# Adding the lower parts of float64 weights by accumulating transfers instead of identity products

## The chip, the cores and the metric

The kernel runs on one core of a Trainium2 chip. A core has a matrix engine (TensorE, PE in the profile), a vector engine (VectorE, DVE), a scalar engine (ScalarE, ACT), a general engine (GpSimd, POOL) and a queue engine that issues transfers (SyncE, SP); 16 DMA engines move the data between DRAM and the on-chip memory SBUF. Each engine takes its instructions in the order of the program and waits on semaphores for the others. PE writes into the accumulators (PSUM); ACT and DVE read them out. The metric is device microseconds (us) of one launch, lower is better.

## The reference

Two attentions in a row, then a gated layer. `q`, `k`, `v` are float32 `[8, 8, 576, 64]` (batch, head, sequence, width), `p` holds 32 packed queries for each head.

```python
p_packed = sm_attn(p, k, v)
out = sm_attn(q, p_packed, p_packed)          # scale 1/8, softmax, 576 x 32 scores for each head
x = out.transpose(0, 2, 1, 3).reshape(8, 576, 512)
h = relu(x @ w_in)                            # w_in  [512, 1024], float64
conv = sum_k conv_w[k] * shift(h, k - 1)      # conv_w [3, 1024], float64, along the sequence
return ((h * sigmoid(conv)) @ w_out).astype(float32)   # w_out [1024, 512], float64
```

The three weights come as float64, since a float32 array was multiplied by a float64 scalar. [...]

## The kernel before, in words

**Tiling.** There are 16 groups `g` of four heads (two to a batch). `attention(g)` runs the first attention on the 32 packed queries of four heads, and the second one with its results. `packed_weight(b, hf)` multiplies the packed results of batch `b` into half `hf` of `w_in`, so that `ffn1(b, j)`, j = 0 to 7, makes 128 of the 1024 channels of `h` straight from the second attention's weights, applies the convolution and the gate, and leaves the result in `hgt`. `ffn2(m)`, m = 0 to 35, multiplies 128 rows of it with `w_out`: 24 products of 512 columns, three for each of 8 chunks.

**Split precision.** The large products run on float32r, a rounded form of float32. Their operands are split into a high part (rounded) and a low part (what the rounding left), and three products high·high, high·low, low·high are added. So `ffn2` needs `wo_hi` and `wo_lo`, and a tile `xhi` and `xlo` of its input; `ffn1` needs `ghi`, `glo` and `a2hi`, `a2lo`.

**The weights.** `w_in` and `w_out` are cut into four tiles each, `weight(0)` to `weight(3)` and `weight(4)` to `weight(7)`, of 128 x 1024 numbers (1 MB as float64). Below, W0 to W7 are these tiles. `load_weight(i)` brings one into a staging area (a part of `hgt[1]`, or `stage`). `f64_parts` then takes the upper words on ACT (line 267), shifts and masks them on DVE (lines 269 and 271) into the main part `t` and the factor `e`, and multiplies the lower words by `e` on DVE (line 273) into `lo`, a part of `wo_lo`. The number is t + lo. Before the change, `lo` has the sign turned, and PE makes the sum: the identity times `t` plus the negative identity times `lo`, and for W4 to W7 also minus `hi`, the rounded copy of `t` that ACT has made on line 318 (line 325, two halves of 512 columns). ACT copies the result out of the accumulators on line 329: to `w_in_sb` for W0 to W3, to `wo_lo` for W4 to W7. Events name the stages: ("wd", i) loaded, ("wp", i) staging free, ("ws", i) scratch in `wo_lo` free, ("w", i) tile ready. `packed_weight(b, 0)` needs W0 and W1, `packed_weight(b, 1)` W2 and W3, and `ffn2(0)` W4 to W7.

**The order.** Each of these functions is a stream of steps; a step is the work of one engine. `ORDER` is a table written out in the source: pairs of base-36 digits, each the number of the stream whose next step is issued. What each engine does, and in what order, is fixed by it. `Flow` walks through the table, with a model of the times of its own, for one purpose alone: where it expects PE to stand idle, it puts idle products of the identity (`warm`, line 243), as long as the first `ffn2` has not been issued. Tokens (`gw`, `x`, `big` and others) stand for buffers and must be free before a step that takes them.

**What the steps before `ffn2(0)` are.** On DVE the table of before has 106 steps ahead of line 679 of `ffn2(0)`: the three steps on lines 269, 271 and 273 for each of W0 to W7, the softmax steps of groups 0 to 3 and the first of group 4, two transposes on line 417, lines 650, 654 and 660 for the eight `ffn1(0, j)`, and line 650 of `ffn1(1, 0)`. On PE they are 76 steps ahead of `ffn2(0)`, the eight of line 325 among them.

Of the kernel before, what the change touches and what calls it, by code (L numbers as in the profile page):

```python
# [18 lines left out]


ORDER = (
    "003k3m04020303040304080b0b04050b0j053k3l06060c0c0j0c0506013q0g06050j0c0e063r0o3u0k0k0r3k3k070e3k0e073k3r3r060906"
    "0k0k0e0f0f3r06060e0m0m3k3k0a06063v3v0r0r3s060s0s3v0e3n0s0m0d3w0i060q3v0e0e0m0s0d0d0e060606060n0h40060d3r3t3t3t0z"
    "0z0m3r0u0u0u0z3x0e3t0n3v3v170e06063t3t0l0l3x0e0m0m3x3y0e0e3x0e0v0e060e0e46460u0u0l0m4641410e410v413x0l0m0p46170m"
    "0m3x3z3z0m170t3z47410w0m0u0e0e423z10471f0t0u0m0m41410t0t470u0u0u0u3z47480m0u0m120u434848121249490u490m144843480u"
    "49434a4a123z4849484a4a490u494a0u444b12453z43454a4a0m4b150x4c4c1f1f4g4c4c124d4b4b43434g4g4c0u4b4d4c4c4d4d4b4b0m0m"
    "4d434g4e4e4d0u0u454d4f4f0u454h4h4h4f4f4e4e454h4f4f4i4i4e4e45184i1a4f4e1c4i1313456e6e4j4j124j0y1a4k4k4k4i4j4k1212"
    "164i4i6e6e4k6f1a6e6e6e6e6e4k6e1n1g1a1a114l6e4l4l6f4j121i4k1i1b1b1a124j4j4l1212191i4m4m1a4m1j4m4m6f4n1a4n3o1l1a6g"
    "6f6f1n6f6f1a4q4n1n124m4l4l6g1a4m4l4n1j121a1d1s1k6f6f6f1v6f6f4o4o1o4n4p4o4o4o124p4p4q204p4p6h4q6h4o6g1i1i6g1v6g6g"
    "1v1a6g6g6g6g4n236g6g12124p4n121q1i1i4r4p1q4o23231a1q1w126i1a1a6i1a121a1a6h6h6h6h6h6h1q1q6h6h4r6h1t1e6h6e1y1y6j1a"  # L30
    "1a1r1r1q1q1y246i6i6i6i6i1h4r4s4s4s4s4t4t2b1m1y6i4t1z4s2b2b291z4t4t6i1y1i1i284s4t2626261y1i1i4u4u6i6i6i4s6j4t4v1y"
    "4v4u4v1p1i1i4v1u3p212j4u4u2c4w2g6k6k1q6j6j6j266j6j6j6j6j4w1q1i4w4w1i1i4u6j262e274u2e4w4w501q1q4v1i4w4v2j2j6k2o6k"
    "6k6k6k2e6l4v2k1q1q6l1y6k4x4x501y6k6k6k6k4y2a271i1i4y4y1x4y4y4z4z1q1q226l6l1y1y262r4z6m6m264x4x4x6l2e2e2r6l6l6l1i"
    "1i1q1q4z4z4x4x1q6l6l512m2r6l4y4z4z4y1q1q6n51501q6m6m6m6l6j6m6m6m6m6m6m6m2h2f26526n6n1y2m2f516n6o52521y2m1y535354"
    "5426546n256n6n6n6o5252521y5454541y52262e2w6n6n5326546p6n555555262d261y26531y5a536o2m566o6o6o26556p55262z2e2e5353"
    "36561y5a556o556o565626566o6o6o5a2e6o6q56566q265757576p1y6p2z6p5758582s582p596p1y59596p6p6p6p572m2657266p2z585858"
    "572n5959595b2e2u2u582m592e262n6q2i6q6q6q6q2u6q2u6q6q6p2x6r6r2e2m375b6q6q2e2e5c5b2l305c5c5c6r375d2e6s5d5d5e6r5e5c"
    "2q2v5d5d375c5e5c5e5d2u5d6r6r6r5e5e2e5e3f6r6r6r2m2m5f5f5f5g5g6s5h2v2m2u325f2e5f2e5g5g2m345g6t6r6r5h6t5f5f6s6s5g5h"
    "6s2u2m5h5h2e6s6s6s6s5g6s6s6s5i5i6t6t5h2e5i2m385i6t6t2m6u6t6t2u2u6t6t322m2m2m2t6u5i5j2m326t5j3f5k5k5j6n6t2e5h5l5l"
    "6v5i2m2m6v335k326u6u6u2m6u6u6u6u6u6u5i5j5j5m5m5j5l5m3f5j326v6v5n5n5n5m3c5m5m5n5n5o5o2y6v5m332u32325o5n3a3a3g3a6v"  # L40
    "5p5p6v6v6v326v5n5o5o6w6w316v5o5q5q3a2u5o3b6w6w6v6u356w6w5r5q3a5p5q32325p5p2u2u3b5q5r6x5r5r5p5p3i5u5q5u3a326w6w6w"
    "6w6w6w6x5r5q395s5s3i325r2u2u2u6y2u6y6x6x6x6x6x6x6x5s6x3i3a3j3j6x6z5t5t5t5s2u5r5s32322u32326y6y6y6y3i6y6y6y6z6y5s"
    "2u3i6y323e3a3a5v3d5v2u5s5t5t5t5u3i3a6z5t6x7032323270326z6z6z6z6z6z6z6z3i5v5w5w5w6z5w5w5x5x5x5x5x5y5y705y3a5y3i3i"
    "705w5x5x71703h5y5w3a717070707070705z6y70605y5z5z5y5z726060713i3i5z5z6064643i3i3a5z7261617171717171613a3a3i717171"
    "717362623a3a3a6160603a613i3i3a723a6072737272727272727263626363636161643i7474633i73737373737373737373653i3i746262"
    "74636274747474637474743i6275666674726667676775686666666667677575756975756565687668687575756867676868766975756969"
    "6a6a6a6b7676696a6a6b6969766a6b6b6b6b6a76767676766c77776c76766d78786c6d6d7777777777777777776b6d6d6d6c6c6c6c6d7779"
    "797878787878787878787979797a7a79797979797a79797b7b7a7a7a787a7a7a7a7a7a7b7b7b7c7c7b7b7b7b7b7b7b7c7c7c7c7c7d7d7c7c"
    "7c7c7c7d7d7d7d7d7d7d7d7d7d"
)  # L50


# [133 lines left out]
def tile_packed_attention_conv_gate(  # L186
# [71 lines left out]
    def f64_parts(tiles, raw, m, after=(), take=(), sets=None):

        pair = raw.rearrange("r (c t) -> r c t", t=2)  # L260
        up = pair[:, :, 1].bitcast(I32)
        low = pair[:, :, 0].bitcast(U32)
# [4 lines left out]
        nc.scalar.activation(out=e, in_=up.bitcast(F32), func=AF.Prelu, scale=F64_REBIAS, alpha=-(2.0**32))  # L267
# [1 line left out]
        nc.vector.tensor_scalar(out=ti, in0=ei, scalar1=3, scalar2=None, op0=ALU.logical_shift_left)
# [28 lines left out]
    def weight(i):  # L298

        c, cols, src, st = weight_tile(i)  # L300
        hi, lo = (w[:, 2 * (i % 4) : 2 * (i % 4) + 2, :].rearrange("r c f -> r (c f)") for w in (wo_hi, wo_lo))
# [8 lines left out]
        after = [("wd", i), "minus"] + ([("ws", i - 4)] if i >= 4 else [])  # L310
        if src.dtype != F32:
            yield from f64_parts(tiles, st, DFF, after, [token], [("wp", i)])
        else:
            yield Step("DVE", 0, after=after, take=[token])
            parts.append((ident, st))
        if i >= 4:
            yield Step("ACT", 905)
            nc.scalar.copy(out=hi, in_=parts[0][1])
# [4 lines left out]
        for hf in range(2):
            for k, (w, x) in enumerate(parts):
                nc.tensor.matmul(  # L325
                    out=s[:, hf, :], lhsT=w, rhs=x[:, 512 * hf : 512 * hf + 512], start=k == 0, stop=k == len(parts) - 1
                )
# [1 line left out]
        nc.scalar.copy(out=w_in_sb[:, c : c + 2, cols] if i < 4 else lo.rearrange("r (c f) -> r c f", c=2), in_=s)  # L329
# [151 lines left out]
    def attention(g):  # L481
        G = grp[g]
        yield Step("PE", 556, after=[("pT", g), ("kT", g)] + [("s1", g - 1)] * (g > 0), take=["big", "a1"], give=["kT", "pT"], sets=[("s1", g)], cols=1152, tiled=True)
        t = score(G["pT"], G["kT"], g)
# [2 lines left out]
        nc.vector.tensor_reduce(out=nm, in_=t[:, :, :SH], axis=AX.XY, op=ALU.max, negate=True)  # L487
# [3 lines left out]
        nc.scalar.activation(
# [70 lines left out]
        G["a2"] = (hi, lo)  # L562

    def sums(g):
        yield Step("DVE", 69, after=[("sm", g)])
# [1 line left out]
        nc.vector.tensor_scalar(out=rs, in0=grp[g]["sm"], scalar1=EPS, scalar2=None, op0=ALU.add)
# [1 line left out]
        nc.vector.reciprocal(out=rs, in_=rs)
# [188 lines left out]
```

## Time and profile before

| | |
|---|---|
| time, median of 2 runs | 421.76 us (421.48 to 422.05) |
| the profiled execution's own time | 422.01 us |
| its span, first to last instruction | 420.2 us |
| PE busy / DVE / ACT / POOL | 410.4 / 343.6 / 316.3 / 1.6 us |
| mean granted clock of PE | 0.994 |
| transfers | 47.21 MB; on the GpSimd queue 0.02 MB |

The span is cut into 40 slices on the profile's page: PE is busy at 90% or more in all but the first and the last, DVE in the third to the 25th at 80% or more and falling behind them, ACT at 90% from about 40 us to 80 us. Matmuls are pipelined and their ends are modelled, so consecutive starts tell more about PE than durations: line 695 has rows of about 400 ns that start 233 ns apart. A row of DVE overlaps the one behind it by about 70 ns in the same way.

### The profile page before, as it was taken

How to read it: one execution, taken by the hardware profiler on the slowest of the kernel's cores; microseconds unless marked ns; L12 is line 12 of the kernel's file. 1: busy time of each engine (PE TensorE's matmuls, PEld its weight loads, DVE VectorE, ACT ScalarE, POOL GpSimd, SP SyncE). 2: the span in 40 equal slices, each digit the busy share in tenths (PEclk: the TensorE clock that was granted, in tenths of full speed). 3: DMA queues.
4: the chain of work that ended last, by engine and by line, in shares of the span. 5: the costliest groups of instructions: out<-in, count | busy, mean ns of one | idle time of the engine just before them, and what ended most of it. 6: DMA issues, size and time to landing. Idle time of an engine off the chain costs nothing.

```text
span 420.2 us, 8196 instructions
## 1 busy us (share of the span) xinstructions
PE 410.4 (98%) x3347; PEld 324.4 (77%) x3347; DVE 343.6 (82%) x488; ACT 316.3 (75%) x505; POOL 1.6 (0%) x13
## 2 busy tenths in 40 slices
...
GB/s 254 381 383 309 181 256 82 43 85 153 100 168 180 112 165 137 81 111 58 129 103 127 27 79 111 2 108 111 56 50 27 25 2 75 27 25 25 51 50 51
DMA packets 135621, 47.21 MB, mean 112 GB/s; under 512 B 119700, under 2 KB 127892, under 8 KB 135584
## 3 DMA queue, kind: packets, MB, share of 16 engines
...
q0 software_dynamic: 32, 0.02, 0.1%
...
## 4 chain that ended last, share of the span: by engine, by line
PE 85%; ACT 4%; DVE 1%; issue 0%; ACTq 0%
PE fo L695 45%; PE big L633 23%; PE sm L695 4%; PE big L444 4%; PE big L581 3%; PE sm L507 2%; PE big L498 2%; PE big L325 1%; ACT hgt L658 0%; ACT wo_lo L329 0%; ACT hbuf L644 0%; PE sm L523 0%; PE idle L243 0%; PE sm L471 0%; ACT L658 0%
## 5 line engine op out<-in xcount | busy, mean ns | idle before, releaser
L695 PE MATMUL fo<-wo_hi,xhi 128*128 128x512 f32 x264 | 107.6, 408 | 0.7 <-ACT o L700 0.7
L695 PE MATMUL fo<-wo_hi,xlo 128*128 128x512 f32 x264 | 104.3, 395 | 0.0
L695 PE MATMUL fo<-wo_lo,xhi 128*128 128x512 f32 x264 | 104.3, 395 | 0.0
L679 DVE TENSOR_TENSOR xlo<-hgt,xhi 128x1024 fp32r<-128x1024 f32 (+1 forms) x40 | 44.0, 1105 | 23.6 <-ACT xhi L676 23.4
L695 PEld LDWEIGHTS fo<-wo_hi,xhi 128*128 128x128 f32 x264 | 49.7, 188 | 15.8 <-ACT o L700 1.9
L650 DVE SCALAR_TENSOR_TENSOR hgt<-hbuf,cw,hgt 128x576 f32<-128x576 f32 x64 | 51.5, 808 | 10.9 <-ACT hgt L648 10.5
L695 PEld LDWEIGHTS fo<-wo_hi,xlo 128*128 128x128 f32 x264 | 49.6, 188 | 11.9
L695 PEld LDWEIGHTS fo<-wo_lo,xhi 128*128 128x128 f32 x264 | 49.7, 188 | 9.1
L633 PE MATMUL big<-a2hi,ghi 128*128 128x288 f32 x256 | 55.8, 299 | 0.0
L633 PE MATMUL big<-a2lo,ghi 128*128 128x288 f32 x256 | 54.8, 295 | 0.0
L633 PE MATMUL big<-a2hi,glo 128*128 128x288 f32 x256 | 54.5, 294 | 0.0
L644 ACT ACTIVATE hbuf<-big 128x576 f32<-128x576 f32 x64 | 41.8, 655 | 14.5 <-PE big L633 13.1
L654 DVE SCALAR_TENSOR_TENSOR hgt<-hbuf,cw,hgt 128x576 f32<-128x576 f32 x64 | 51.7, 810 | 1.1
L658 ACT ACTIVATE hgt<-hgt 128x576 f32<-128x576 f32 x64 | 43.2, 684 | 10.6 <-DVE hgt L654 10.5
L660 DVE TENSOR_TENSOR hgt<-hgt,hbuf 128x576 f32<-128x576 f32 x64 | 47.4, 748 | 4.6 <-ACT hgt L658 4.4
L648 ACT ACTIVATE hgt<-hbuf,cw 128x576 f32<-128x576 f32 x64 | 49.5, 778 | 1.0
L700 ACT COPY o<-fo 128x512 f32<-128x512 f32 x33 | 19.4, 587 | 36.9 <-PE fo L695 31.0
L633 PEld LDWEIGHTS big<-a2hi,ghi 128*128 128x128 f32 x256 | 42.2, 188 | 6.1 <-issue 0.9
L633 PEld LDWEIGHTS big<-a2hi,glo 128*128 128x128 f32 x256 | 41.0, 188 | 0.0
L633 PEld LDWEIGHTS big<-a2lo,ghi 128*128 128x128 f32 x256 | 40.9, 188 | 0.0
L676 ACT CAST xhi<-hgt 128x1024 fp32r<-128x1024 f32 (+1 forms) x40 | 38.2, 961 | 2.5 <-DVE hgt L660 1.6
L487 DVE TENSOR_REDUCE nm<-big 128x1 f32<-128x576 f32 x16 | 12.0, 749 | 14.9 <-PE big L444 14.8
...
## 6 DMA issues: line engine op xcount, KB each, us to landing
out_dram<-o SPq DMA_DIRECT2D x36, 256.0 KB, 2.2
...
hgt<-in_moe_w_in_dram SPq DMA_DIRECT2D x3, 1024.0 KB, 11.3
hgt<-in_moe_w_out_dram SPq DMA_DIRECT2D x3, 1024.0 KB, 7.5
...
```

The costliest lines, as they stand in the source:

```text
L444: nc.tensor.matmul(out=o.rearrange("c (j r) -> c j r", r=NR) if by_block(g) else o, lhsT=lhs[r, 32 * i : 32 * i + 32], rhs=rhs[r, :, h, :] ...
L633: nc.tensor.matmul(out=t[:, hf, :SH], lhsT=w[:, gg, js], rhs=x[:, hf * SH : (hf + 1) * SH], start=n == 0, stop=n == 3 * NG - 1,)
L644: nc.scalar.activation(out=h[:, 1 : S + 1].rearrange("c (f s) -> c f s", f=2), in_=t[:, :, :SH], func=AF.Relu)
L648: nc.scalar.activation(out=d, in_=h[:, 1 : S + 1], func=AF.Copy, scale=cw[:, NJ + j : NJ + j + 1])
L650: nc.vector.scalar_tensor_tensor(out=d, in0=h[:, 0:S], scalar=cw[:, j : j + 1], in1=d, op0=ALU.mult, op1=ALU.add)
L654: nc.vector.scalar_tensor_tensor(out=d, in0=h[:, 2 : S + 2], scalar=cw[:, 2 * NJ + j : 2 * NJ + j + 1], in1=d, op0=ALU.mult, op1=ALU.add)
L658: nc.scalar.activation(out=d, in_=d, func=AF.Sigmoid)
L660: nc.vector.tensor_tensor(out=d, in0=d, in1=h[:, 1 : S + 1], op=ALU.mult)
L676: nc.scalar.copy(out=hi[:, :, o], in_=src)
L679: nc.vector.tensor_tensor(out=lo[:, :, o], in0=src, in1=hi[:, :, o].bitcast(F32), op=ALU.subtract)
L695: nc.tensor.matmul(out=t, lhsT=x[:, c, :], rhs=w[:, c, :], start=c + i == 0, stop=c == NJ - 1 and i == 2)
L700: nc.scalar.copy(out=o, in_=t)
```

## The change

The sum t + lo is made by a transfer that the GpSimd queue issues, from SBUF to SBUF, which adds `lo` to what lies at its destination (512 KB of it for each tile). `lo` keeps its sign. For W0 to W3, `t` is written straight into `w_in_sb`, the transfer adds `lo` to it there, and nothing else is to be done. For W4 to W7, `t` lies in the `xhi` buffer; behind the transfer ACT makes `hi` from it, and a new step on DVE makes `lo = t - hi`. The PE steps of line 325 and the ACT copies of line 329 go. The order table is a new one (1521 steps where there were 1525), with two added rules on who must be issued before whom in `attention` and `sums`. `w_in` tiles W1 and W0 are now loaded in the order W1, W0, ahead of the first `v`.

```diff
 ORDER = (
...
+    ACCUMULATE = 3000
...
-        nc.vector.scalar_tensor_tensor(... scalar=2.0**-52 if rest.dtype == F32 else -(2.0**-52), ...)
+        nc.vector.scalar_tensor_tensor(... scalar=2.0**-52, ...)
...
         def tiles():
-            t, e = (wk.tile([128, DFF], F32, name="tmp", tag=tag) for tag in tags)
-            parts.extend([(ident, t), (minus, lo)])
-            return t, e, lo
+            t, e = (wk.tile([128, DFF], F32, name="tmp", tag=tag) if i >= 4 or tag == tags[1] else None for tag in tags)
+            whole.append(pair(t) if i >= 4 else w_in_sb[:, c : c + 2, cols])
+            return whole[0], pair(e), pair(lo)
+
         if src.dtype != F32:
-            yield from f64_parts(tiles, st, DFF, after, [token], [("wp", i)])
+            yield from f64_parts(tiles, st, DFF, after, [token], [("wp", i)], pair)
+            yield Step("POOL", ACCUMULATE, give=[token] * (i < 4), sets=[("ws", i)] + [("w", i)] * (i < 4))
+            nc.gpsimd.dma_start(out=whole[0], in_=pair(lo), accum_op=ALU.add)
...
         if i >= 4:
-            yield Step("ACT", 905)
-            nc.scalar.copy(out=hi, in_=parts[0][1])
-            parts.append((minus, hi))
-        ns = 2 * (864 + 234 * (len(parts) - 1))
-        yield Step("PE", ns, take=["big"], give=[token], sets=[("ws", i)], cols=2 * (1536 + 512 * len(parts)))
-        s = big()
-        for hf in range(2):
-            for k, (w, x) in enumerate(parts):
-                nc.tensor.matmul(
-                    out=s[:, hf, :], lhsT=w, rhs=x[:, 512 * hf : 512 * hf + 512], start=k == 0, stop=k == len(parts) - 1
-                )
-        yield Step("ACT", 905, give=["big"], sets=[("w", i)])
-        nc.scalar.copy(out=w_in_sb[:, c : c + 2, cols] if i < 4 else lo.rearrange("r (c f) -> r c f", c=2), in_=s)
+            yield Step("ACT", 905, after=after)
+            nc.scalar.copy(out=pair(hi), in_=whole[0])
+            yield Step("DVE", 1135, give=[token], sets=[("w", i)] + [("wp", i)] * (src.dtype == F32))
+            nc.vector.tensor_tensor(out=pair(lo), in0=whole[0], in1=pair(hi).bitcast(F32), op=ALU.subtract)
```

Read as steps, the new table does this. On PE the same 68 other steps stand ahead of `ffn2(0)`, and one more, the transpose of line 471 for group 7. On DVE 109 steps stand ahead of line 679 of `ffn2(0)`: those of before without line 650 of `ffn1(1, 0)`, and the four new subtractions. On ACT the eight copies of line 329 and line 601 of `packed_weight(1, 1)` are gone from ahead of line 676 of `ffn2(0)`, and three short steps have come there (lines 468, 518 and 526). The GpSimd queue gets eight transfers, in the order W0, W1, W2, W3, W5, W4, W6, W7. The loads on SP begin with k0, p0, p1, k1, q0, W1, W0, v0, where they began with k0, p0, q0, k1, v0, W0 (the letter is the array, the number the group or tile).

More of the change, by code (lines that the diff above doesn't have):

```diff
@@ L27 @@
[L27 to L46, printed above, removed]
@@ L47 @@
-    "6a6a6a6b7676696a6a6b6969766a6b6b6b6b6a76767676766c77776c76766d78786c6d6d7777777777777777776b6d6d6d6c6c6c6c6d7779"
-    "797878787878787878787979797a7a79797979797a79797b7b7a7a7a787a7a7a7a7a7a7b7b7b7c7c7b7b7b7b7b7b7b7c7c7c7c7c7d7d7c7c"
-    "7c7c7c7d7d7d7d7d7d7d7d7d7d"
+    "003m3k3n08030403030b040404023s3q0105063k3k3k06063u3k3k0c060c0b0g0b0c3r063k0c3k0e0e090j0j3t0a0o050i050e0j3r3r073t"
+    "073r3v3v060606050e0k3w0h0e06060k0f0k0f3v3v0k0d0d3r0m0606063t0m3t3t3v0d0d0e3l0r0e0e0s0e0e0e0e06060m0m0r3x0l0s400r"
@@ new lines @@
+    "0l0z0z0z0m0s0s0u3x3x0e0606060e0n0n0e060e0l3x0e3x0e0m0m0m0m0l3y0646460646460m0p0q0u0e0e0u0m0w0e0v0m0m41410v480m0m"
+    "410m4848484949174a4a4a41413z0m0m484a0m49423z17170m3z470t0u0t0u4a3z0m493z0t0u0u10440u0t0u0u0u474747490u0x41410u12"
+    "1f1f1243430u0u121243490u13434348140u49483z3z4a4b1f1n4b4b4c0u4a0u454c4b134b4c454b4c454b4c45454d4g4g4d4e124g4d4d4c"
+    "4c4f4d43434e4g4e4e4d4d4f0u4f4h4h12124h124e4e4f0u4f4i4e4545124f4f4j0y1c3o4i4i186e6e4k4j4k4k6f4j1a1n4i1a4i4i6f1a4k"
+    "4k1n4k154i114j1g1b6e6e6e6e6e6e6e6e1a1a4l6e4h4l4j164k1l1s4j1v1k6g4l1a12121i1i1i121b6f6f6g4l4j124l6f6f1a196f4m1a1a"
@@ new lines @@
+    "4m124m4m124l4m1j4l6f6f6f4n1v4n1v6f4q1a6f1d4m4n6g6g4o4o4o124m4n1a121j124n121o4o4o1i1i6g4p234p6g6g6g6g6g4p4p4p6h4o"
+    "4n6g6g6h1a4q4p1q1q1i1i4o4n4r1q1a4p1w6h1a1a6h6h6h6h1e1q6h6i6i1a1q12121a1a2023236h6h6h6h1t2g1a6j1a4r4q1q1y1a1r1r1y"
+    "1y6i6i6i6i6i4s4s246j4t1q4s4r4s1h1z6i1i1m4t1i2b4t4t4s4t4u1y1y4u2b2b6i6i6i4u1z6i6k2128261y264u1i1i4u1i1i4s4s1p4t4u"
+    "4u6k266j6j6j6j6j6j4v272j4v1y4v4v2c4v6j266j6e1u4w1i4t6j264w4w6l1i1i1i6l1i1i4w6k6k1q1q296k2e2e1q4w6k6k6k6k1q2j6k4v"
+    "4v1i2j1y1y6k226k4w3p4x4x4x2e1x2k1q6l6l6l6l1y1y506m264x1q501q4x271q4w1q1i6m4y6l6l2r6l4z504x4y4y4y2f1q1q4z2o6j6l2e"
@@ new lines @@
+    "6l4z2m51514z4y4y2m4z262e4z2a1q4x4z6m1q1q4y512f6m6m6m6m26266m6m6m2r526n6n6m6m6l2r526o53251y545352521y5454262e5254"
+    "26542m2p526n6n2s6n6n6n6n6n54532e2z6n52541y6n6o261y2h266p551y5353552m5656262655551y6p55565353566o2z2z6o6o6o6o6o6o"
+    "2u2e2e6o556o575757371y1y566q2d551y566p6n2w6o262u2n6q6p6p6p6p2i583758562m37586p6p592n59596p6p261y265758585757585a"
+    "5a595958575959265a5b2m2m5b6r6r26266q6q6q6q6q6q6q2e2e6q302e2u6s6s5c5c5d5c5c6q5e5d5d6q6p5d5c6r6r2m6r6r5e6r5e5e5e2e"
+    "2u6r5c5c6r6r5e2e5d5b5e6r6r5f2l2m5f2v2v2u5g5g5f5f2e6t32322m2m2u5k5f6s5d6s5k6s5d6s2m6s2m6s6t6s5f6s2m5k2m5f2e2e2e6s"
@@ new lines @@
+    "5h325g5g5g6u2x2q6t6t2e6t2m5h6t335h6u5g5g2m6t6s6t6t5i2e6t6t6v6t5j2e5h5h2m342m6v5i2u6u6u6u6u6u5h5j5j5j5i5j5h3f2m2m"
+    "5i2y5i2u5l2u5j5j6u6u3f32325i5m5m5m6u6u5i38335n6u5m5m5n5n5n5o6v3c5m5m6v6v5n5p2t6w5l5o3f5l5o32323a5p5o5p5n3a5o3e5o"
+    "3a5n5p6w5o2u32326v6v6v5q5q5q6v6v6v5p2u5p3b2u3g316x5r5r5r6v5q5q6w6w6w6w5p5r5r356x2u3a3a6w6w6w6w5s6w5s5r3d6w6y3i32"
+    "5u3a325s2u5r3i3i6y3232326x6x6x5s6x6x6x5t6x6x2u5s363b3j2u32395q3a5s5t5u5v3j3i6x5s6x3a5u3a5t3i6z6y6y6y2u2u2u5t5t6y"
+    "6y6y6y6y3i32322u6z2u6y3a6z32323i5t325q5t705v3h6z6z6z6z6z6z6z323i703a3a3i6z6z6y5w5x715w5w5y5y715w5w5w5w5y5y5y5y5x"
@@ new lines @@
+    "5x705y7070707070705z5z5z7070705x5v5x5z5z725z3i3a3i647164605x5z3a64726071717171713i3a3a3a3i606071715x607161717361"
+    "3i3i73603i616061727272723i727272727262633a3a743i61623a6263636165623a3i3i7373733i73737373737273736174636262636266"
+    "7474746363667566666666656766746874747474676868756874686769696967676768766569696875757575757575757569756a676a6a76"
+    "696b6a6b6a6a6a776b6b76766c6c7676767676777676766d6c6c787877776b77776d6d776d7777776d6d6b77776c6c6c6b78787878786d79"
+    "79787878787a7a797978797979797979797b7b7a7a7a7a7a7a79747a7a7a7a7c7c7b7b7b7b7b7b7b7b7b7b7c7c7c7d7c7c7d7c7c7c7c7c7d"
@@ L50 @@
+    "7d7d7d7d7d7d7d7d7d"
 )
@@ L256, in small, with f64_parts @@
         return ps.tile([128, 512], F32, name=tag, tag=tag)
[L258 to L262, printed above, removed]
+    def f64_parts(tiles, raw, m, after=(), take=(), sets=None, shape=lambda ap: ap):
+        words = raw.rearrange("r (c t) -> r c t", t=2)
+        up = shape(words[:, :, 1]).bitcast(I32)
+        low = shape(words[:, :, 0]).bitcast(U32)
         yield Step("ACT", 93 + m * 14 // 15, after=after, take=take)
@@ L275, in f64_parts @@
             in0=low,
-            scalar=2.0**-52 if rest.dtype == F32 else -(2.0**-52),
+            scalar=2.0**-52,
             in1=e,
@@ L302, in weight, with pair @@
         token, tags = ("gw", ("ghi", "glo")) if i < 2 else ("x", ("xhi", "xlo"))
-        parts = []
+        after = [("wd", i)] + ([("ws", i - 4)] if i >= 4 else [])
+        whole = []
+        def pair(ap):
+            return ap.rearrange("r (c f) -> r c f", c=2)
         def tiles():
-            t, e = (wk.tile([128, DFF], F32, name="tmp", tag=tag) for tag in tags)
-            parts.extend([(ident, t), (minus, lo)])
-            return t, e, lo
-        after = [("wd", i), "minus"] + ([("ws", i - 4)] if i >= 4 else [])
+            t, e = (wk.tile([128, DFF], F32, name="tmp", tag=tag) if i >= 4 or tag == tags[1] else None for tag in tags)
+            whole.append(pair(t) if i >= 4 else w_in_sb[:, c : c + 2, cols])
+            return whole[0], pair(e), pair(lo)
@@ L311, in weight @@
         if src.dtype != F32:
-            yield from f64_parts(tiles, st, DFF, after, [token], [("wp", i)])
-        else:
-            yield Step("DVE", 0, after=after, take=[token])
-            parts.append((ident, st))
+            yield from f64_parts(tiles, st, DFF, after, [token], [("wp", i)], pair)
+            yield Step("POOL", ACCUMULATE, give=[token] * (i < 4), sets=[("ws", i)] + [("w", i)] * (i < 4))
+            nc.gpsimd.dma_start(out=whole[0], in_=pair(lo), accum_op=ALU.add)
+        elif i < 4:
+            yield Step("ACT", 905, after=after, sets=[("wp", i), ("ws", i), ("w", i)])
+            nc.scalar.copy(out=w_in_sb[:, c : c + 2, cols], in_=pair(st))
+        else:
+            whole.append(pair(st))
@@ L487, in attention @@
         nc.vector.tensor_reduce(out=nm, in_=t[:, :, :SH], axis=AX.XY, op=ALU.max, negate=True)
-        yield Step("ACT", 731, give=["big"], sets=[("sm", g)], table="exp")
+        yield Step("ACT", 731, after=[("rs", g - 2)] * (g > 1), give=["big"], sets=[("sm", g)], table="exp")
         a1 = wk.tile([128, S], F32, name="a1", tag="a1", bufs=1)
```

9 lines of the change are left out of this document (2 added, 7 removed).

## The prediction

> **What bounds the kernel now.** I read the page, then busy times by stretch. Columns of the stretches: the stretch, its length, busy us (instructions) of PE, PE's weight loads, DVE, ACT, POOL, the granted clock, DMA share, GB/s.
>
> ```profile
> span 420.2 us, 8196 instructions
> PE 410.4 (98%) x3347; PEld 324.4 (77%) x3347; DVE 343.6 (82%) x488; ACT 316.3 (75%) x505; POOL 1.6 (0%) x13
> ...
> 0.00:10.00 10.00, 5.65 (x34) 4.89 (x36) 0.00 (x0) 3.62 (x9) 1.58 (x13) 0.96 0.81 253
> 10.00:20.00 10.00, 9.87 (x127) 7.82 (x126) 4.28 (x13) 7.90 (x17) 0.00 (x0) 0.87 1.04 383
> ...
> 18.00:83.00 65.00, 63.93 (x650) 44.05 (x643) 63.28 (x100) 62.89 (x104) 0.00 (x0) 1.00 0.86 216
> ...
> 84.50:417.00 332.50, 331.35 (x2561) 267.67 (x2559) 276.43 (x381) 242.22 (x379) 0.00 (x0) 1.00 0.44 81
> ```
>
> The 98% of PE invites the reading that what is taken from PE is gained. The stages say otherwise. From 84.5 us, where `ffn2(0)` begins, to the end, PE alone is full (332.5 - 331.35 = 1.15 us idle), and DVE has 56 us to spare. Between 18 and 83 us three engines are full together: PE lacks 1.1 us, DVE 1.7, ACT 2.1. All of line 325 lies there. The chain of waits (start, us, what) shows the lead passing from engine to engine:
>
> ```profile
> 43.04 0.69 DVE s L531
> 43.73 0.59 DVE tmp L269
> ...
> 47.60 0.90 ACT wo_lo L329
> ...
> 61.50 0.90 ACT wo_lo L329
> ...
> 66.94 2.66 PE big L325 x8
> ...
> 77.75 2.66 PE big L325 x8
> ```
>
> So the span is two pieces: the time at which `ffn2(0)` starts, and PE's work from there. The second piece is hardly touched: decoded, the new table has the same PE steps ahead of `ffn2(0)`, less line 325, plus one transpose. The question is when `ffn2(0)` starts.
>
> **PE and ACT: what goes.** PE in the groups (busy us, mean ns), and two starts of W2's tile:
>
> ```profile
> L325 PE MATMUL big<-tmp,ident 128*128 128x512 f32 x32 | 16.6, 602 | 0.0
> L325 PE MATMUL big<-wo_lo,minus 128*128 128x512 f32 x16 | 12.8, 798 | 0.0
> L243 PE MATMUL idle<-ident 128*128 128x128 f32 x58 | 9.7, 306 | 2.5 <-POOL ident masks.py:199 2.5
> L325 PE MATMUL big<-wo_hi,minus 128*128 128x512 f32 x8 | 3.2, 398 | 0.0
> ...
> 30.05 1.13 PE L325 MATMUL big<-tmp,ident 128*128 128x512 f32 x2
> ...
> 32.35 1.02 PE L325 MATMUL big<-tmp,ident 128*128 128x512 f32 x2
> ```
>
> These overlap, so I take occupation: a `w_in` tile 32.35 - 30.05 = 2.3 us, a `w_out` tile 2.66 us (chain). 4 x 2.3 + 4 x 2.66 = 19.8 us leave PE. ACT loses the eight copies of line 329, 0.90 us each in the chain: 7.2 us. Both engines stop being the tightest, and where PE waits it waits, or runs more idle products of line 243.
>
> **DVE: what is added.** The steps ahead of line 679 of `ffn2(0)` are a floor, since DVE takes them in order:
>
> ```profile
> 13.99 0.16 DVE L567 TENSOR_SCALAR rs<-sm 128x1 f32<-128x1 f32 x1 [1.58 <-ACT a L491]
> ...
> 17.78 0.14 DVE L569 RECIPROCAL rs<-rs 128x1 f32<-128x1 f32 x1
> ...
> 18.09 0.67 DVE L269 TENSOR_SCALAR tmp<-tmp 128x1024 int32<-128x1024 int32 x1
> ...
> 81.61 0.81 DVE L650 SCALAR_TENSOR_TENSOR hgt<-hbuf,cw,hgt 128x576 f32<-128x576 f32 x1
> 82.34 0.15 DVE L567 TENSOR_SCALAR rs<-sm 128x1 f32<-128x1 f32 x1
> ...
> 82.81 1.23 DVE L679 TENSOR_TENSOR xlo<-hgt,xhi 128x1024 fp32r<-128x1024 f32 x1
> 83.95 0.75 DVE L487 TENSOR_REDUCE nm<-big 128x1 f32<-128x576 f32 x1
> ```
>
> From W0's first shift (18.09) to `ffn2(0)` (82.81) are 64.72 us. The four new subtractions have line 679's shape and take 83.95 - 82.81 = 1.14 us each: +4.56. Line 650 of `ffn1(1, 0)` moves behind: -(82.34 - 81.61) = -0.73. The two small steps of group 0's `sums` (13.99 and 17.78) move behind W0's shift: about +0.2 with their overlap. Sum +4.0, so 68.7 us, with the 1.7 us of idle kept.
>
> Nothing earlier makes room. W0's shift needs W0:
>
> ```profile
> hgt<-in_moe_w_in_dram SPq DMA_DIRECT2D x1, 1024.0 KB, 11.3
> ...
> 3.90 1.89 SPq L296 DMA_DIRECT2D hgt<-in_moe_w_in_dram  x1
> ...
> 16.33 1.18 ACT L267 ACTIVATE tmp<-hgt 128x1024 f32<-128x1024 f32 x1
> ```
>
> It lands at 3.90 + 11.3 = 15.2 us. The new order of the loads puts p1 and W1 ahead of it and takes v0 away: 128 + 1024 - 576 = 576 KB more, at the 383 and 253 GB/s of the first two stretches 1.5 to 2.3 us. So 16.7 to 17.5; before, ACT came to it 1.1 us after it landed (16.33), now at once. The first shift follows at 16.7 + 1.2 = 17.9 to 18.7. I take 18.1, as before.
>
> **The sum.** Line 679 of `ffn2(0)` then starts at 18.1 + 68.7 = 86.8 us, 4.0 later. PE's side of that place, and the transpose that the table moves ahead of it:
>
> ```profile
> 62.67 0.27 PE L471 MATMUL sm<-ident,pm 128*128 128x128 f32 x1
> 62.87 1.09 PE L581 MATMUL big<-w_in_sb,ppT 64*32 64x512 f32 x16
> ...
> 84.49 0.48 PE L695 MATMUL fo<-wo_hi,xhi 128*128 128x512 f32 x1
> ...
> 85.04 0.40 PE L695 MATMUL fo<-wo_hi,xlo 128*128 128x512 f32 x1
> ```
>
> Before, PE reached its first product with `xlo` at 85.04, 1.0 us after DVE had made it (82.81 + 1.23 = 84.04); PE, not DVE, held the start. That margin is used up, all but some 0.1 us for the signal: PE is 4.0 - 0.9 = 3.1 us later. The transpose (62.87 - 62.67 = 0.2 us) leaves the second piece. Net +2.9 us on the profiled 422.01: 424.9. The median of before is 0.25 under its profiled run, so I forecast **424.7 us**: nearly 20 us less on PE buy nothing, and the four subtractions come through as a small loss.
>
> **The transfers, which the trace of before doesn't show.** A step of POOL waits for DVE's line 273, and only later transfers stand behind it. Behind the waiting consumers stand, for W0 and W1, PE's `packed_weight(0, 0)` and all that follows it; for W4 to W7 ACT's line 318 and the `ffn1` and softmax steps after it, then DVE's subtraction and everything after that. The nearest rows:
>
> ```profile
> out_dram<-o SPq DMA_DIRECT2D x36, 256.0 KB, 2.2
> ...
> stage<-in_moe_w_in_dram SPq DMA_DIRECT2D x1, 1024.0 KB, 13.6
> ...
> s<-in_moe_conv_w_dram POOLq DMA_DIRECT2D x1, 24.0 KB, 5.7
> ...
> L336 POOL DMA_DIRECT2D s<-in_moe_conv_w_dram x1: 652/652/652, 1.4 to 1.4; - x1
> ```
>
> Lower end 2.2 us (half the bytes, quiet engines), upper end 13.6 (1 MB from DRAM among others, and an addition must read 512 KB twice over). I take 6, near the one row of the GpSimd queue, 5.7 for little data among other loads. The Trainium skill, "DMA: Bandwidth & Descriptors", section "Anatomy of one DMA", gives about 2.0 us plus bytes over 436 GB/s, an estimate of 3.2 us here; the sum would be the same, as the cover below is then not even half used.
>
> The cover is what the tables put between a tile's line 273 and its use:
>
> ```profile
> L650 DVE SCALAR_TENSOR_TENSOR hgt<-hbuf,cw,hgt 128x576 f32<-128x576 f32 x64 | 51.5, 808 | 10.9 <-ACT hgt L648 10.5
> L660 DVE TENSOR_TENSOR hgt<-hgt,hbuf 128x576 f32<-128x576 f32 x64 | 47.4, 748 | 4.6 <-ACT hgt L658 4.4
> ...
> L318 ACT CAST wo_hi<-tmp 128x1024 fp32r<-128x1024 f32 x4 | 4.3, 1074 | 0.0
> ```
>
> For W7 DVE has eleven steps there: six of lines 650 and 654 (0.81), three of line 660 (0.75), W6's subtraction (1.14), line 561 (taken as line 660's 0.75): 9.0 us, less 11 overlaps of 0.07, 8.2. ACT's copy takes 1.07 of it: 7.1 us for the transfer. So at 6 us it costs nothing.
>
> **Rivals.** (1) *The cover is too short.* If a transfer takes more than 7.1 us, DVE stands still at W7's subtraction; the same can happen at W5's copy on ACT and at `packed_weight(0, 0)`, whose covers I take as equal. At 10 us that is 3 x 2.9 = 8.7, 433.4 us; at 13.6, 3 x 6.5 = 19.5, 444 us: slower. For it: the DMA share is 0.86 from 18 to 83 us, and the large loads take up to 13.6. Against: these wait in SP's one line, and the transfers have a queue of their own. Chance 0.15.
>
> (2) *DVE is held by the GpSimd queue's own work.* The issue of 24 rows took 0.65 us; at worst 128 rows take 128 / 24 as long, 3.5 us. If lines 269 and 271 can't run meanwhile, the table puts five of them within 3.5 us of a tile's line 273: W2's two directly behind W0's, W1's mask and W3's pair some 2 us behind, W4's shift 3 us: at worst 3.5 + 1.5 + 1.5 + 0.5 = 7, 431.7 us. The Trainium skill, "SBUF — State Buffer", section "Who interferes with whom", states that such two-port steps of VectorE and GpSimd's writing of descriptors lock each other out; no row here shows it, as the one issue, at 1.4, was over before DVE began (0.00 busy to 10 us). Chance 0.05, half of it under 2%.
>
> (3) *DVE's gaps close.* W0 lands earlier, or the 1.7 us of idle go, with PE and ACT less full: 3 to 5 us less, 420 to 422. For it: 7.2 us less on ACT, which led the chain between 47 and 62 us. Chance 0.13.
>
> (4) *PE is the bound after all*, and its 19.8 us come off: 402 us. DVE's floor forbids it, unless its steps become shorter. Chance 0.02.
>
> The forecast keeps 0.64; 0.01 is for what I do not see, and counts as faster below.
>
> **How the numbers follow.** A measurement of this kernel tells about 2% from no change, 413.3 and 430.2 us. Faster is (4) with the unseen: 0.03. Slower is (1), half of (2): 0.17. The rest, 0.80, is within. The range runs from 419.5, the better end of (3), to 433, which takes in (2) and the cheap half of (1); (4) and the dear half of (1), about 0.1, are left out with some of the unforeseen.
>
> **What would show it.** Right: line 325 gone, some 20 us more of idle products and waits on PE ahead of `ffn2(0)`; that at 85 to 89 us; DVE without gaps from 18 us on; the transfers landing within 7 us. Wrong: gaps on DVE behind line 318 or line 593 that end with a transfer (1); lines 269 and 271 longer than 0.7 us (2); `ffn2(0)` before 80 us (4), or PE idle behind it by more than 3 us, which no step of mine has.

## The result, and the profile after

The changed kernel takes 432.68 us (432.67 to 432.68, two runs) where the kernel before takes 421.76: a ratio of 1.026, interval 1.0215 to 1.0303. The profiled execution took 432.67 us. Line numbers of the new kernel are one higher or lower than before: lines 269, 271 and 273 are now 270, 272 and 274, line 318 (the rounded copy) is 326, line 679 is 678, line 695 is 694, line 243 is 244. New are line 318 (the transfer) and line 328 (the subtraction). In the experiments, lines behind a part that is left out stand a few numbers lower.

From the page of the changed kernel: busy times, one group, and the two rows of transfers on the GpSimd queue (count, KB each, median us from issue to landing).

```profile
span 430.7 us, 8529 instructions
...
PE 418.4 (97%) x3513; PEld 339.2 (79%) x3513; DVE 348.2 (81%) x492; ACT 312.2 (72%) x499; POOL 10.1 (2%) x21
...
L244 PE MATMUL idle<-ident 128*128 128x128 f32 x280 | 39.1, 290 | 2.6 <-POOL ident masks.py:199 2.6
...
w_in_sb<-wo_lo POOLq DMA_DIRECT2D x4, 512.0 KB, 11.3
tmp<-wo_lo POOLq DMA_DIRECT2D x4, 512.0 KB, 6.4
```

PE got no emptier: what line 325 left was filled with idle products, 280 where there were 58, 39.1 us busy where it was 9.7. The transfers land in 11.3 us (W0 to W3) and 6.4 us (W4 to W7) by the median.

Busy time by stretch, the columns as in the prediction: from W0's first shift to line 678 of `ffn2(0)`, and from `ffn2(0)` on.

```profile
19.80:92.71 72.91, 69.64 (x805) 57.07 (x804) 67.61 (x105) 57.38 (x101) 8.46 (x8) 1.00 1.03 237
...
94.00:427.00 333.00, 331.51 (x2559) 267.21 (x2559) 276.93 (x382) 244.02 (x379) 0.00 (x0) 1.00 0.43 82
```

The steps of DVE in the first stretch, with the gap ahead of each and what ended it, and PE's first product of `ffn2(0)`:

```profile
19.80 0.68 DVE L270 TENSOR_SCALAR w_in_sb<-tmp 128x1024 int32<-128x1024 int32 x1
...
34.09 0.69 DVE L270 TENSOR_SCALAR w_in_sb<-tmp 128x1024 int32<-128x1024 int32 x1 [1.22 <-ACT tmp L268]
...
46.20 0.78 DVE L530 STREAM_TRANSPOSE s<-big 128x576 f32<-128x576 f32 x1 [2.25 <-PE big L443]
...
64.95 1.23 DVE L328 TENSOR_TENSOR wo_lo<-tmp,wo_hi 128x1024 fp32r<-128x1024 f32 x1 [0.39 <-ACT wo_hi L326]
...
92.71 1.19 DVE L678 TENSOR_TENSOR xlo<-hgt,xhi 128x1024 fp32r<-128x1024 f32 x1
...
94.00 0.48 PE L694 MATMUL fo<-wo_hi,xhi 128*128 128x512 f32 x1
```

`ffn2(0)` starts at 94.00 us where it started at 84.49, and this +9.5 is nearly the whole loss: the span is 10.5 us longer. Line 678 stands at 92.71 instead of 82.81, +9.9, and the two stretches divide that: the first shift is later by 19.80 - 18.09 = 1.7; DVE has 67.61 - 63.00 = 4.6 us more work; and its idle time in the stretch is 72.91 - 67.61 = 5.3 where it was 1.7, so 3.6 more. Behind `ffn2(0)` PE is as full as before (1.5 us idle in 333 us).

The chain of waits (start, us, what) shows what held the start and what the largest gap followed:

```profile
2.75 7.46 DMA hgt<-in_q_dram
...
12.36 2.46 PE idle L244 x22
...
16.17 2.21 PE idle L244 x18
18.37 0.73 PE big L443 x16
...
30.90 11.58 DMA w_in_sb<-wo_lo
42.48 0.04 issue
42.52 1.06 PE big L580 x8
```

The transfer of W1 is issued at 30.90 and lands 11.6 us later; `packed_weight(0, 0)` on PE (line 580) waits for it, and the 2.25 us gap of DVE at 46.20 follows behind that.

### The profile page after: what moved, and what is told of

It reads as the page before. It is cut to its first block, busy times and chain, and to the rows that moved or that the text cites. A ratio compares the mean times of both kernels' runs of the same rounds, so it can differ in the third digit from the quotient of the medians.

```text
span 430.7 us, 8529 instructions
## 1 busy us (share of the span) xinstructions
PE 418.4 (97%) x3513; PEld 339.2 (79%) x3513; DVE 348.2 (81%) x492; ACT 312.2 (72%) x499; POOL 10.1 (2%) x21
## 4 chain that ended last, share of the span: by engine, by line
PE 91%; DMA 4%; DVE 2%; ACT 0%; SPq 0%; issue 0%; ACTq 0%
PE fo L694 44%; PE big L632 24%; PE idle L244 6%; PE big L443 4%; PE sm L694 4%; PE big L580 4%; DMA w_in_sb<-wo_lo 3%; PE sm L506 2%; PE big L497 2%; DMA hgt<-in_q_dram 2%; DVE wo_lo L274 1%; PE big L427 1%; PE big L596 1%; DVE tmp L272 1%; DVE w_in_sb L270 0%; PE sm L522 0%
## 5 line engine op out<-in xcount | busy, mean ns | idle before, releaser
L694 PEld LDWEIGHTS fo<-wo_hi,xhi 128*128 128x128 f32 x264 | 49.7, 188 | 19.2 <-issue 4.5
L244 PE MATMUL idle<-ident 128*128 128x128 f32 x280 | 39.1, 290 | 2.6 <-POOL ident masks.py:199 2.6
L699 ACT COPY o<-fo 128x512 f32<-128x512 f32 x33 | 19.2, 583 | 30.4 <-PE fo L694 25.3
L244 PEld LDWEIGHTS idle<-ident 128*128 128x128 f32 x280 | 35.1, 200 | 7.3 <-issue 3.9
## 6 DMA issues: line engine op xcount, KB each, us to landing
w_in_sb<-wo_lo POOLq DMA_DIRECT2D x4, 512.0 KB, 11.3
```

The costliest lines, as they stand in the source:

```text
L244: nc.tensor.matmul(out=t[:, :128], lhsT=ident, rhs=ident, start=True, stop=True)
L694: nc.tensor.matmul(out=t, lhsT=x[:, c, :], rhs=w[:, c, :], start=c + i == 0, stop=c == NJ - 1 and i == 2)
L699: nc.scalar.copy(out=o, in_=t)
```

## The experiments

My first theory: the transfers, slow among the loads, cost the part that the prediction had at nothing, and the four subtractions cost what it said. Rivals: the subtractions cost nothing and the order alone does it; the idle products on PE hold the work up; or the transfers cost by what they do to the loads, not by the waits for them.

**Without the transfers.** Line 318 goes; the order and everything else stays.

```diff
-            nc.gpsimd.dma_start(out=whole[0], in_=pair(lo), accum_op=ALU.add)
```

> Leaves out the eight accumulating transfers: the lower parts are computed but not added; order, idle products, DVE steps as in the changed kernel. Theory of the sum (ffn2(0) starts 9.8 us later than before: 1.7 us from a later first shift of W0, 4.0 from the steps added on DVE, 4.2 from new gaps on DVE, most of them behind transfers): only the gaps behind the transfers go, packed_weight(0,0) no longer waits for a landing; 3 to 4 us less than the changed kernel, 428.5 to 430. Rival 'the landings are all of it': back to 422. Rival 'the new order alone': no change, 432.7.

429.50 us, ratio 1.0175 (1.0153 to 1.0198): 3.2 us less than the whole change, not all 10.9. PE's `packed_weight(0, 0)` in this kernel:

```profile
40.63 1.09 PE L579 MATMUL big<-w_in_sb,ppT 64*32 64x512 f32 x16
```

It runs in one piece at 40.63, while in the changed kernel its second half starts only at 42.52 and its end comes 1.9 us later (43.58 against 41.72); DVE's gap behind it is 0.54 us instead of 2.25. The 0.39 us ahead of the first subtraction is there without transfers too. So the transfers cost something, and here the wait for W1 is the largest part of it, but more than half of the loss is there without them.

**Without the subtractions.** Line 328 goes.

```diff
-            nc.vector.tensor_tensor(out=pair(lo), in0=whole[0], in1=pair(hi).bitcast(F32), op=ALU.subtract)
```

> Leaves out the four new subtractions on DVE (line 328), so that the low parts of W4 to W7 lack what the rounding left; all else as in the changed kernel. Theory of the sum: DVE is the floor of the stage, each us taken from it comes off: 4 x 1.14 = 4.6 us less, 428.1. Rival 'the landings are all of it': the freed time turns into waits, 431.5 to 432.7.

432.95 us, ratio 1.0266 (1.0248 to 1.0284): no gain at all. DVE has 4 us less to do, and line 677 of `ffn2(0)` stands at the same place, since the time comes back as gaps:

```profile
75.24 0.82 DVE L648 SCALAR_TENSOR_TENSOR hgt<-hbuf,cw,hgt 128x576 f32<-128x576 f32 x1 [1.97 <-ACT hgt L646]
...
84.54 0.82 DVE L648 SCALAR_TENSOR_TENSOR hgt<-hbuf,cw,hgt 128x576 f32<-128x576 f32 x1 [0.83 <-ACT hgt L646]
...
92.72 1.23 DVE L677 TENSOR_TENSOR xlo<-hgt,xhi 128x1024 fp32r<-128x1024 f32 x1 [0.35 <-ACT xhi L674]
```

DVE's work is therefore not the only floor. PE is full of idle products up to 95 us here, a number fixed when the program was built; that was the next suspect.

**Without the idle products**, the function that issues them returning at once:

```diff
-        t = ps.tile([128, 512], F32, name="idle", tag="fo")
-        for _ in range(n):
-            nc.tensor.matmul(out=t[:, :128], lhsT=ident, rhs=ident, start=True, stop=True)
+        return
```

> Leaves out all idle products of line 244 (280 of them in the changed kernel, 58 before); all else as in the changed kernel. Theory of the sum: they fill waits; what they hold up is some 1.3 us at the first transposes of attention(0), where they end at 14.8 us while ACT was done at 13.4: 431 to 432, unless the granted clock falls, and then slower than 432.7. Rival 'the idle products hold PE' (they make 24% of the chain of waits of the first 105 us): 427 or less.

434.43 us, ratio 1.0289 (1.0272 to 1.0306): 1.8 us more. The stretch from 50 to 70 us shows the likely reason (the eighth value, 0.68, is the granted clock):

```profile
50.00:70.00 20.00, 11.74 (x122) 6.44 (x121) 18.37 (x26) 14.36 (x25) 1.73 (x2) 0.68 0.95 212
```

PE is idle 8 us of 20 and its clock falls; what the idle products took is given back as slower products. This kernel can't separate the two.

**The transfers of W0 to W3 led elsewhere**, into a buffer that POOL zeroes first, so that nobody waits for them.

```diff
-            nc.gpsimd.dma_start(out=whole[0], in_=pair(lo), accum_op=ALU.add)
+            if i < 4:
+                nc.gpsimd.memset(pair(hi).bitcast(F32), 0.0)
+            nc.gpsimd.dma_start(out=whole[0] if i >= 4 else pair(hi).bitcast(F32), in_=pair(lo), accum_op=ALU.add)
```

> The transfers of W0 to W3 add into a part of wo_hi that is set to zero and not used until later, instead of w_in_sb; so packed_weight waits for none of them, while the same bytes move at the same time (the lower parts of w_in are thereby not added); W4 to W7 as in the changed kernel. Theory of the sum: what counts of these four transfers is the wait of packed_weight(0,0), so this is as fast as without any transfers, within 1 us: 429 to 430.5. Rival 'the transfers slow the loads': less than half of the gain without transfers remains.

432.71 us, ratio 1.0245 (1.0227 to 1.0263): no change. DVE's gap behind `packed_weight(0, 0)` shrinks to 0.55 us, and the one at W3's shift grows from 1.22 to 1.90. But the zeroing is no neutral addition: beside it W3's shift took 1.00 us instead of 0.69 and one mask of line 272 even 2.20, and DVE was busy 69.2 us in its first stretch instead of 67.6. It hints that something else stands ready when the wait for W1 goes; it isn't clean.

**Half the idle products, and the parts once more.** Half of them keep the mean granted clock at 0.99 to 1.00 and let PE move. Four kernels: the whole change so; without the subtractions; without the subtractions and the transfers; without the transfers.

```diff
-        for _ in range(n):
+        for _ in range((n + 1) // 2):
```

> The changed kernel with half of each run of idle products (140 groups of two instructions become about 75). Without the subtractions the time did not move (432.95), and PE had no gap from 50 us to ffn2(0): its queue holds a number of idle products fixed at build, so a gain on DVE is lost there. Theory 'two floors' (DVE's steps with the subtractions, and PE's steps with the idle products, both end at the same place): shortening PE's alone gives 0 to 1 us, 431.5 to 432.7. Rival 'PE's idle products alone hold the stage': 428 or less. If the granted clock falls below 0.99 the run tells nothing.

> Half of the idle products, and the four subtractions of line 328 left out (low parts of W4 to W7 lack what the rounding left). Theory 'two floors': now the 4.6 us of DVE come off, 428 to 429. Rival 'DVE's added steps never mattered': as e5, within 1 us.

> Half of the idle products, and neither subtractions nor transfers (lower parts not added, low parts of W4 to W7 incomplete): what stays is the new order with the steps that both kernels have, less PE's sums and ACT's copies. Theory 'two floors' with the transfers' 3.2 us of e1: 424 to 425.5, the 1.7 us of the later first shift and little else. Rival 'the new order is worse by itself': 427 or more.

> Half of the idle products, transfers left out (lower parts not added), subtractions kept. Theory 'two floors': as without transfers (429.5), DVE's steps being the floor: 428.5 to 429.5. Rival 'PE's idle products hold the stage': 426 or less.

| half the idle products, and | us | ratio (interval) | first shift | line 678 | DVE busy / idle between | `ffn2(0)` |
|---|---|---|---|---|---|---|
| all of the change | 432.39 | 1.0261 (1.0225 to 1.0297) | 18.79 | 92.77 | 67.56 / 6.42 | 94.00 |
| no subtractions | 431.28 | 1.0221 (1.0196 to 1.0246) | 18.34 | 91.64 | 63.61 / 9.69 | 93.00 |
| no transfers | 427.65 | 1.0150 (1.0123 to 1.0177) | 18.46 | 87.28 | 67.08 / 1.74 | 88.48 |
| neither | 426.38 | 1.0113 (1.0087 to 1.0139) | 17.82 | 85.80 | 63.26 / 4.72 | 87.16 |

The theory of two floors holds for the first kernel and misses the other three. Three things follow. The transfers cost 432.39 - 427.65 = 4.7 us; line 678 is 5.5 us later with them, and 4.7 of that is idle time of DVE (6.42 against 1.74). The subtractions cost 1.1 to 1.3 us and not the 4 that they take on DVE: without them the idle time grows by 3. And with neither, with DVE's work of before and less on PE and ACT, the kernel is still 4.6 us slower than before (3.7 between the two profiles). That part belongs to the new order: DVE idles 4.72 us between the two points where it idled 1.72, and the piece behind `ffn2(0)` is 1.0 us longer (423.9 - 87.16 against 420.2 - 84.49).

DVE's gaps of the first of the four, and the two steps of ACT that ended the first and the last of them:

```profile
34.25 0.69 DVE L270 TENSOR_SCALAR w_in_sb<-tmp 128x1024 int32<-128x1024 int32 x1 [1.85 <-ACT tmp L268]
...
42.91 0.76 DVE L560 TENSOR_TENSOR a2lo<-a2t,a2hi 128x576 fp32r<-128x576 f32 x1 [1.11 <-ACT a2hi L558]
...
71.06 1.23 DVE L328 TENSOR_TENSOR wo_lo<-tmp,wo_hi 128x1024 fp32r<-128x1024 f32 x1 [0.22 <-ACT wo_hi L326]
...
89.66 1.23 DVE L328 TENSOR_TENSOR wo_lo<-tmp,wo_hi 128x1024 fp32r<-128x1024 f32 x1 [1.14 <-ACT wo_hi L326]
...
33.09 1.12 ACT L268 ACTIVATE tmp<-hgt 128x1024 f32<-128x1024 f32 x1 [2.62 <-DMA hgt<-in_moe_w_in_dram]
...
88.58 1.05 ACT L326 CAST wo_hi<-tmp 128x1024 fp32r<-128x1024 f32 x1 [1.51 <-DMA tmp<-wo_lo]
```

At 34.25 DVE stands because ACT waited 2.62 us for W3's load, an ordinary load of the SP queue, and the 1.11 at 42.91 comes from the same delay by way of ACT and PE. At 71.06 and 89.66 it stands because of transfers, W4's for 0.22 us and W7's for 1.14. Without the transfers the first and the last two are gone and the second is 0.19. PE doesn't wait for W1 here: line 580 runs in one piece at 41.67, as all that leads to it is late already. So a new theory: some three fifths of the price (1.85 + 1.11 - 0.19 of 4.7) are paid at a load that the transfers slow, three tenths (1.14 + 0.22) at W4 and W7.

**Nobody waits for W0 to W3, second try.** As the first of the four, but the four transfers add `lo` to itself, with no zeroing.

```diff
-            nc.gpsimd.dma_start(out=whole[0], in_=pair(lo), accum_op=ALU.add)
+            nc.gpsimd.dma_start(out=whole[0] if i >= 4 else pair(lo).bitcast(F32), in_=pair(lo), accum_op=ALU.add)
```

> As e5 (half of the idle products, 432.4), but the transfers of W0 to W3 add lo onto lo itself instead of w_in_sb (the lower parts of w_in are not added): the same bytes at the same time, and packed_weight waits for none of them. Theory 'the wait of packed_weight(0,0) for the landing of W1 (11 us) is what costs': as e8 without transfers (427.7), within 1 us. Rival 'the loads are slowed': the load of W3 lands as late as in e5 (DVE's shift of W3 not before 33.5 us) and 430 or more.

432.46 us, ratio 1.0237 (1.0196 to 1.0279), against 432.39: with `packed_weight` waiting for none of these four, the price of the transfers is still there. The large gaps stay where they were:

```profile
33.46 0.69 DVE L270 TENSOR_SCALAR w_in_sb<-tmp 128x1024 int32<-128x1024 int32 x1 [1.71 <-ACT tmp L268]
...
42.16 0.76 DVE L560 TENSOR_TENSOR a2lo<-a2t,a2hi 128x576 fp32r<-128x576 f32 x1 [1.15 <-ACT a2hi L558]
...
88.78 1.23 DVE L328 TENSOR_TENSOR wo_lo<-tmp,wo_hi 128x1024 fp32r<-128x1024 f32 x1 [1.26 <-ACT wo_hi L326]
```

The transfers of the stretch from 20 to 35 us show the mechanism. First the kernel without transfers and half the idle products, then this one (queue: packets, MB, share of the 16 engines; then the issues: count, KB each, median us to landing):

```profile
q1 hardware_dynamic: 2514, 5.42, 104.0%
...
hgt<-in_moe_w_in_dram SPq DMA_DIRECT2D x1, 1024.0 KB, 8.2
v<-in_v_dram SPq DMA_DIRECT2D x2, 512.0 KB, 10.2
stage<-in_moe_w_out_dram SPq DMA_DIRECT2D x1, 1024.0 KB, 10.6
...
q<-in_q_dram SPq DMA_DIRECT2D x1, 576.0 KB, 11.2
```

```profile
q1 hardware_dynamic: 2193, 4.36, 82.8%
q0 software_dynamic: 178, 0.66, 22.2%
...
wo_lo<-wo_lo POOLq DMA_DIRECT2D x3, 512.0 KB, 10.2
hgt<-in_moe_w_in_dram SPq DMA_DIRECT2D x1, 1024.0 KB, 10.5
v<-in_v_dram SPq DMA_DIRECT2D x2, 512.0 KB, 16.2
stage<-in_moe_w_out_dram SPq DMA_DIRECT2D x1, 1024.0 KB, 16.8
...
q<-in_q_dram SPq DMA_DIRECT2D x1, 576.0 KB, 21.5
```

The 16 engines are full in both. Where the transfers take 22% of them, the loads get 83% instead of 104%, and each lands later: W3 by 2.3 us, the `v` of this stretch by 6, `q` by 10. W3's load is the first that somebody waits for. In the first kernel of the table, where the transfers go to `w_in_sb`, it is the same: 19.2% and 86.6%, and W3's load takes 10.9 us. So the destination of the transfers doesn't make the difference.

**W1 ahead of W2 on DVE.** Three steps of W1 and three of W2 change places in the table (half the idle products), so that W1's transfer goes out at 24 us instead of 30.

```diff
-    "073r3v3v06...0k0f0k0f3v3v0k0d0d3r0m0606063t0m3t3t3v0d0d0e..."
+    "073r3v3t06...0k0f0k0f3t3t0k0d0d3r0m0606063v0m3v3v3v0d0d0e..."
```

> As e5 (half of the idle products), with DVE's mask and product of W1 ahead of all of W2's instead of behind them, so that W1's transfer is issued some 5 us earlier; the whole computation. Theory 'the landing of W1 holds packed_weight(0,0)': the transposes behind it on DVE come 1 to 2 us earlier, 430 to 431.5. Rival 'the loads are slowed': no change, 432 to 433.

432.50 us, ratio 1.0242 (1.0207 to 1.0276): no change. W3's load is in time for DVE here, and the next load is not:

```profile
37.62 0.65 PE L506 MATMUL sm<-v,a1T 128*32 128x64 f32 x32 [0.75 <-DMA v<-in_v_dram]
40.13 0.44 PE L506 MATMUL sm<-v,a1T 64*32 64x64 f32 x8 [1.86 <-DMA v<-in_v_dram]
```

PE waits 2.6 us for `v`. The share of the engines that the transfers take is paid by whichever load is needed first.

**The kernel before, without line 325 and line 329.** Its own order, with `t` of W0 to W3 written straight to `w_in_sb`, and the sums left out.

```diff
...
-        s = big()
-        for hf in range(2):
-            for k, (w, x) in enumerate(parts):
-                nc.tensor.matmul(...)
-        nc.scalar.copy(out=w_in_sb[:, c : c + 2, cols] if i < 4 else lo.rearrange("r (c f) -> r c f", c=2), in_=s)
```

> The kernel before, its order and its idle products, without the sums on PE (line 325) and without ACT's copies of them (line 329): t goes straight to w_in_sb, the lower parts are not added, the low parts of W4 to W7 lack what the rounding left. Nothing is put in their place, so this is what taking 19.8 us from PE and 7.2 us from ACT is worth at most in that order. Theory (DVE's steps are the floor, ffn2(0) can start 0.8 us earlier at most): 420.5 to 421.7. Rival 'PE is the bound': 402 to 410.

423.79 us (421.88 to 426.37), ratio 1.0033 (1.0008 to 1.0058). The stretch from the first shift to line 677:

```profile
16.17:84.54 68.37, 51.95 (x622) 38.66 (x621) 62.61 (x99) 56.87 (x96) 0.00 (x0) 0.88 0.85 214
```

PE has 11.7 us less to do in it, ACT 5.9, and nothing is gained, not even the 0.1 to 1.3 us that the theory allowed: DVE idles 5.8 us of 68.4 instead of 1.7, and the granted clock is 0.88 instead of 1.00. The fall of the clock is part of that, as this kernel has few idle products; how much, this run doesn't say.

**The kernel before with half its idle products**, as a control for the halving.

```diff
-        for _ in range(n):
+        for _ in range((n + 1) // 2):
```

> The kernel before with half of each run of idle products (29 groups become about 15). Theory: PE held ffn2(0) by 0.8 us over DVE there, so 0 to 0.8 us less, 421 to 422. Rival 'the idle products cost as they do in the changed kernel without transfers' (1.9 us): 420.

422.12 us, ratio 0.9996 (0.9979 to 1.0013): no change. So the halving gains nothing in the order of before, and the rows of the table can be held against the time of before. None of the kernels beats the one before.

## Why the prediction was right and wrong

The time came 8.0 us above the forecast, 0.3 us inside the upper end of the range. That it lies inside is luck: the range reached so far only for rivals (1) and (2), and half of the loss or more is there without any transfer. A slowdown this clear had a chance of 0.17. The reading of the bound was right; the price of the transfers, the start of the first stretch and part of the reason for its length were not.

**Right: PE's and ACT's relief is worth nothing.** The kernel before without line 325 and its copies gains nothing (1.0033), with PE idle 16 us of the first stretch, though at a lower clock; and in the changed kernel the freed time is idle products and waits. "PE is the bound after all" falls. Right too was the hinge: 9.5 of the 10.5 us lie ahead of `ffn2(0)`, and PE has 1.5 us idle behind it, under the 3 that would have spoken against the forecast. The second piece is 1.0 us longer (430.7 - 94.00 against 420.2 - 84.49) where I had 0.2 less; that stays open.

**Wrong: "So at 6 us it costs nothing."** This is the step that failed. Both halves of it did. The landing: 5.7 to 14.5 us in the changed kernel, 10.0 by the median, where I took 6. The row I leaned on, 5.7 us for 24 KB, comes from the start of the kernel. The DMA share of 0.86 from 18 to 83 us was an average: in the kernel before, the engines are full where the first transfers will run (the share is the last value but one, 1.05), and 0.77 from 40 to 80 us.

```profile
20.00:35.00 15.00, 14.68 (x161) 8.91 (x158) 14.13 (x23) 13.28 (x27) 0.00 (x0) 1.00 1.05 365
```

The price: 3.2 us in the changed kernel, 4.7 with half the idle products. The rule of the Trainium skill, "DMA: Bandwidth & Descriptors", section "Anatomy of one DMA", which gave an estimate of 3.2 us, isn't what these runs show: the shortest landing of an accumulating transfer here was 5.1 us.

**Rival 1 had the event, but not its main road.** It had transfers overrunning a cover at W7, W5 and `packed_weight(0, 0)`. In the changed kernel only the last of these waits: `packed_weight(0, 0)` for W1 (1.9 us later, by the run without transfers). ACT copies W7 there 6.3 us after the issue (88.37 against 82.03), without a wait. With half the idle products W7's transfer was issued at 80.86 and asked for at 87.07, when ACT began to wait: 6.2 us against my 7.1, and a landing of 7.7 cost 1.5 us on ACT, 1.14 on DVE; W4 cost 0.2, W5 nothing. So that cover was sized well. And where the wait for W1 is gone, a slowed load holds the same place: W3's with half the idle products and with the transfers led elsewhere, `v` where W1 goes first. Rival 1's 433.4 us for landings of 10 us is close to what came (10.0 and 432.68) by luck, as it had 8.7 us from three covers. What I had not thought of is the other direction: the transfers slow the loads. That the loads slow the transfers too is likely but not shown, as no run has a transfer without loads beside it: in the changed kernel W0 to W3, beside the most loads, landed in 10.2 to 14.5 us, W4 to W7 in 5.7 to 9.7. My argument against the rival, "the transfers have a queue of their own", was wrong in just this: the queue is its own, the 16 engines are not.

**Half right: DVE as the floor.** With half the idle products and no transfers, DVE needs 68.82 us from the first shift to line 678, where the prediction's sum was 68.7, and `ffn2(0)` stands at 88.48, 4.0 later than before, where it had 3.1. The size is right and the reason only in part: without the subtractions the stretch is still 67.98 us, as DVE's idle time rises from 1.74 to 4.72 us (1.7 us of the rise at lines that wait for ACT, 0.9 at one that waits for PE, well ahead of the first subtraction). The subtractions fill waits that the new table has anyway. "The 1.7 us of idle kept" was an assumption about a table I had only counted, not walked through. Rival 3, fewer gaps on DVE, falls: they grew from 1.7 to 5.3 us in the changed kernel.

**Wrong: "I take 18.1, as before."** The first shift stood at 19.80. I followed W0's load alone. The chain of after begins with the load of `q0`, which the new order of the loads puts behind p1 and k1: PE's first product with it starts at 10.26 us, at 8.92 before. DVE comes to the shift only behind group 1's maximum, which waits for PE, and PE has some 4.7 us of idle products in that piece of the chain. With half of them the shift stands at 18.79 (17.8 to 18.8 in the six kernels of the new order with half, 19.8 to 20.6 in the four with all), and that gain is lost at W3's load: line 678 stands at 92.77.

```profile
8.92 1.11 PE L428 MATMUL big<-ident,hgt 128*128 128x128 f32 x5 [1.43 <-DMA hgt<-in_q_dram]
...
10.26 0.76 PE L427 MATMUL big<-ident,hgt 128*128 128x128 f32 x5 [1.26 <-DMA hgt<-in_q_dram]
```

(The first row is of the kernel before, the second of the changed one.)

**Rival 2, DVE held by the GpSimd queue, falls.** Lines 270 and 272 stay at 0.65 to 0.70 us, but for one:

```profile
23.38 1.39 POOL L318 DMA_DIRECT2D w_in_sb<-wo_lo  x1 [20.82 <-DVE wo_lo L274]
...
23.85 0.81 DVE L272 TENSOR_SCALAR tmp<-w_in_sb 128x1024 int32<-128x1024 int32 x1
```

It runs inside the 1.39 us in which POOL issues W0's transfer, and is 0.12 us longer; where `lo` is added to itself, the same step beside an issue of 1.23 us keeps its 0.68. The issues took 0.85 to 1.71 us, where I had 3.5 at worst. If that is the lock of the Trainium skill, "SBUF — State Buffer", section "Who interferes with whom", it costs this kernel a tenth of a microsecond, not 7.

**Put together**, with half the idle products on both sides (spans 419.4, 425.3, 430.4): the new order with the subtractions +5.9, the transfers +5.1 (by the medians +5.5 and +4.7). The prediction had +2.9 for the one and 0 for the other. What it would take to keep the order of before and still use transfers wasn't tried.
